# Gated linear attention and a GELU layer pair: the first rows through two hardware DMA queues, the weights behind a gate

## The chip, the cores and the metric

The kernel runs on one NeuronCore of a Trainium2 chip. The metric is the device time of one execution in microseconds (us), taken as the median over repeated runs. Engines are named as in the profile: PE (TensorE matmul) and PEld (its weight loads), DVE (VectorE), ACT (ScalarE), POOL (GpSimd) and SP (SyncE, which here only issues DMAs).

## The reference

A recurrent, gated linear attention is followed by two dense layers with a tanh GELU between them. B = 4 batches, H = 8 heads, S = 768 steps, D = 48; the layers go 384 to 2048 to 384. Inputs and output are float32.

```python
def _attn_ref(q, k, v, alpha):
    state = zeros(B, H, D, D); y = zeros_like(q)
    for t in range(S):
        state = alpha[:, :, t, :, None] * state + einsum('bhd,bhe->bhde', k[:, :, t], v[:, :, t])
        y[:, :, t] = einsum('bhd,bhde->bhe', q[:, :, t], state)
    return y

def reference(q, k, v, alpha, moe_w_in, moe_w_out):
    x = attn_out.transpose(0, 2, 1, 3).reshape(B * S, H * D)
    h = x @ moe_w_in
    g = 0.5 * h * (1.0 + tanh(sqrt(2 / pi) * (h + 0.044715 * h**3)))
    return g @ moe_w_out
```

## The kernel before

**Tiling.** The 768 steps are cut into 6 chunks of 128, and the 4 batches into 2 pairs, which gives 12 pairs (chunk, two batches), numbered 0 to 11 in the order of the chunks. For each pair four inputs are loaded: a (the decays alpha), q, k and v. One such load of one input is called a row here; it is 128 partitions by 16 heads by 48 numbers, 384 KB of float32 read in runs of 192 bytes. The v rows and the weights are cast to bfloat16 on the way, which the kernel does in DMAs of the software queue, issued by POOL.

**A pair's work.** ACT takes the logarithm of a (ln, L243). PE sums it over the steps (cum, L254 and L256), and ACT makes exp of the sum (b), of its negative (binv) and of its last row (bend). DVE scales q with b (qp) and k with binv (kp, L280). PE transposes both (qkT_ps, L291), they are copied to qkT (L305), and PE forms the scores (at, L327), which DVE masks (atm, L334). The product of kp and v (kv) updates the state (st). PE makes y from scores, v and state (yps), which is copied (x, L383), transposed (xT_ps, L390) and copied into xT (L394). Pairs 8 to 11 use DMA transposes instead of PE.

**The two layers.** For each pair, PE makes 16 groups of hT from w_in and xT (layer 1, L400), ACT applies the GELU (gT, L406), and PE sums over w_out into acc (layer 2, L414). The result is copied to ot (L421) and stored by SP (L426). Layer 1 of pair 0 is the first consumer of the weights. The groups of the two layers go in one fixed sequence (`stream`).

**What sets the order.** The program is scheduled by hand. `tasks` declares every step as a task with an engine, an estimated cost from the table `W`, a priority and its inputs and buffers; `Scheduler.order` then plays these through, always taking the task that can start first (within 60 ns, the one of the best priority), and the result is the fixed order of instructions on each engine. So a change of the loads' estimates also reorders the compute instructions. Where PE would idle in the first 60 us of that plan, a fill of matmuls on zeros is put in (L209). Tiles have numbered buffers in `BUFS`; `ca` is a single PSUM buffer that holds first cum and then the scores of each batch, so they take turns.

**The loads before.** `LOADS` lists the order: rows of pair 0, rows of pair 1, four parts of w_in, four parts of w_out, then the rows of pairs 2 to 11 (pair 2 in two halves). Only a of pair 0 is issued by SP, on a hardware queue; all the rest go through the software queue in this order. At most eight of the software loads are in flight, since each of eight semaphores is used again after its load has landed. `make_upper_triangular` (ut_h) and `make_identity` (ident) are built on POOL after its first and second load. `act_set` loads ACT's function table as ACT's first instruction.

Of the kernel before, what the change touches and what calls it, by code (L numbers as in the profile page):

```python
# [7 lines left out]
F32 = mybir.dt.float32  # L8
# [3 lines left out]
LN_EXP, GELU = 6, 0  # L12


W = dict(
    ln=760, exp=720, bend=170, gelu4=510, gelu2=340, table=1290,
    cum=530, t8=450, t4=225, attn=340, kv=170, inter=170, intra=205, tx=168, l1_4=655, l1_2=340, l2=655,
    qk2=910, qk1=500, ev8=650, ev4=350, mask=640, st=1400, st0=700, xc=520, xe=330, ot=540,
    ev8_act=960, ev4_act=520, xc_act=450, xe_act=450, ot_act=450,
    strip=2120, cast=1500, weight=1850, dma=2100, issue=1100, wissue=760, sp=100, store=2600, turn=1250, landed=2200, xbar_qk=1500, xbar_x=1000, first=3470, cold=500, fill=216, zero=1100,  # L20
)
LAT = {"SP": 0, "PE": 210, "ACT": 110, "DVE": 90, "POOL": 0}

# [1 line left out]
class Task:  # L25


    def __init__(self, kind, cost, prio, emit, deps=(), table=None, land=None, stream=None, xbar=0, late=0):
        self.kind, self.cost, self.prio, self.emit = kind, cost, prio, emit
        self.deps, self.takes = list(deps), []  # L30
        self.table, self.land, self.stream, self.xbar = table, land, stream, xbar
        self.late = late
        self.end = self.done = None
# [102 lines left out]
class _Kernel:  # L136
# [3 lines left out]

    SPLIT = (2,)
    EARLY = (0, 1)
    LOADS = ("0", "1", "in 0", "in 1", "in 2", "in 3", "out 0", "out 1", "out 2", "out 3",
             "2", "3", "4", "5", "6", "7", "8", "9", "10", "11")

    TURN_QK, TURN_X = (8, 9, 10, 11), (8, 9, 10, 11)
    BUFS = dict(ca=1, yk=2, ff=4, la=3, qp=4, kp=4, b8=2, qkT=4, atm=6, x=3, ot=6, bend=8,
                a=4, q=4, k=4, v=6)

    def __init__(self, ctx, tc, q, k, v, alpha, w_in, w_out, out):  # L150
        nc = self.nc = tc.nc
        self.tc, self.out = tc, out
        B, H, S, D = q.shape
        self.B, self.H, self.S, self.D = B, H, S, D
        C = self.C = 128
        self.NCH = S // C
        self.src = {"a": alpha, "q": q, "k": k, "v": v}
        self.w_in_dram, self.w_out_dram = w_in, w_out
        self.d_model, self.d_ff = w_in.shape
        self.NKT, self.NFT = self.d_model // C, self.d_ff // C  # L160

        self.const = ctx.enter_context(tc.tile_pool(name="const", bufs=1))
        self.sb = ctx.enter_context(tc.tile_pool(name="sb", bufs=1))
        self.ps = ctx.enter_context(tc.tile_pool(name="ps", bufs=1, space=bass.MemoryType.PSUM))

        const = self.const
        self.ut_h = const.tile([C, C], F16, name="ut_h")
        self.ut = const.tile([C, C], BF16, name="ut")
        self.ident = const.tile([C, C], BF16, name="ident")
        self.ones = const.tile([C, 1], F16, name="ones")  # L170
        self.zero = const.tile([C, 512], BF16, name="zero")
        self.w_in = const.tile([C, self.NKT, self.d_ff], BF16, name="w_in")
        self.w_out = const.tile([C, self.NFT, self.d_model], BF16, name="w_out")
        self.state = [[const.tile([C, H // 2, 2 * D], BF16, name=f"st{b}_{i}") for i in range(2)]
                      for b in range(B)]
        self.ring = {n: [const.tile([C, 2, H, 64], F16 if n == "la" else BF16, name=f"{n}{i}")
                         for i in range(self.BUFS[n])] for n in ("la", "qp", "kp")}
        self.used = {n: 0 for n in self.ring}
        self.xT = [const.tile([C, self.NKT, B, C], BF16, name=f"xT{c}") for c in range(self.NCH)]
        self.NG = 2  # L180
        self.gT = [const.tile([C, self.NFT, B * C], BF16, name=f"gT{i}") for i in range(self.NG)]
        self.eng = {"ACT": nc.scalar, "DVE": nc.vector}
# [30 lines left out]
    def load(self, n, c, i, lo=0, hi=2):  # L213

        nc, C, H, D = self.nc, self.C, self.H, self.D
        u = self.p[c, i]

        def emit(e):
            if n not in u:
                u[n] = self.tile(n, [C, 2, H, D], BF16 if n == "v" else F32)  # L220
            src = self.src[n][2 * i + lo:2 * i + hi].rearrange("b h s d -> s (b h) d")[c * C:(c + 1) * C]
            (nc.sync if e == "SP" else nc.gpsimd).dma_start(u[n][:, lo:hi].rearrange("t b h d -> t (b h) d"), src)  # L222
        return emit

    def load_w(self, which, part):
        def emit(e):
            if which == "in":
                w = self.d_ff // 4
                sl = slice(part * w, (part + 1) * w)
                self.nc.gpsimd.dma_start(  # L230
                    self.w_in[:, :, sl], self.w_in_dram.rearrange("(j c) n -> c j n", c=self.C)[:, :, sl])
            else:
                w = self.NFT // 4
                sl = slice(part * w, (part + 1) * w)
                self.nc.gpsimd.dma_start(
                    self.w_out[:, sl, :], self.w_out_dram.rearrange("(n c) p -> c n p", c=self.C)[:, sl, :])
        return emit
# [191 lines left out]
    def tasks(self):  # L429
        s = self.s = Scheduler(self.BUFS, self.fill, 60000)  # L430
# [3 lines left out]
        pairs = list(self.p)  # L434


        loads, n = {}, 0

        def load(key, cost, emit):
            nonlocal n  # L440
            land = W[{"v": "cast", "w": "weight"}.get(key[0], "strip")]
            loads[key] = s.add("load", {"POOL": cost}, n, emit, land=land // 2 if key[0] != "w" and key[1] in self.SPLIT else land)
            n += 1

        def rows(m, names="aqkv"):
            for lo, hi in self.parts(m):
                for r in names:
                    load((r, m, lo), W["issue"] * (hi - lo) // 2, self.load(r, *pairs[m], lo, hi))
                    loads[r, m, hi - 1] = loads[r, m, lo]

        def weights(which, parts):
            for part in map(int, parts):
                load(("w", which, part), W["wissue"], self.load_w(which, part))

        loads["a", 0, 0] = loads["a", 0, 1] = s.add("load", {"SP": 400}, 0, self.load("a", 0, 0), land=W["first"])
        for step in self.LOADS:
            if step == "0":
                rows(0, "qkv")
            elif step.isdigit():
                rows(int(step))  # L460
            else:
                weights(*step.split())
# [3 lines left out]
        for m, (c, i) in enumerate(pairs):  # L466
            u, P = self.p[c, i], 100 * m
# [3 lines left out]
            for lo, hi in self.parts(m):  # L471
                n = hi - lo
# [10 lines left out]
                step = 1 if early else n  # L483
# [12 lines left out]
            for j in range(2):  # L496
                b, o = 2 * i + j, P + 10 + 3 * j
                k = kp[j]
                if m not in self.TURN_QK:
                    turned = []  # L500
                    for which in ("q", "k") if early else ("qk",):
                        n = 4 * len(which)
                        cost = {"DVE": W[f"ev{n}"]}
# [42 lines left out]
        n = 0  # L546
# [45 lines left out]
    def run(self):  # L592
        nc = self.nc
        self.tasks()
        self.act_set(LN_EXP)
        nc.vector.memset(self.zero, 0.0)  # L596
        nc.vector.memset(self.ones, 1.0)
        first = [lambda: make_upper_triangular(nc, self.ut_h, val=1.0, diag=True), lambda: make_identity(nc, self.ident)]
        for i in range(max(self.BUFS[n] for n in self.ring)):
            for n in self.ring:  # L600
                if i < self.BUFS[n]:
                    nc.vector.memset(self.ring[n][i][:, :, :, self.D:64], 0.0)
        for b in range(self.B):
            for i in range(2):
                nc.vector.memset(self.state[b][i], 0.0)
        order = self.s.order()
        for t in order:
            if t.load == LN_EXP:
                self.act_set(LN_EXP)
            t.emit(t.engine)  # L610
            if t.kind == "load" and t.engine == "POOL" and first:
                first.pop(0)()
                if not first:
                    nc.vector.tensor_copy(self.ut, self.ut_h)
# [30 lines left out]
```

## Time and profile before

| | |
|---|---|
| median of 9 runs | 188.61 us (188.43 to 188.75) |
| the profiled execution | 188.43 us |
| its span in the profile | 186.7 us |
| PE busy | 175.4 us (94%) |
| ACT, DVE, POOL busy | 131.8, 104.3, 63.7 us |
| software DMA queue | 32464 packets, 19.27 MB |
| hardware DMA queue | 17296 packets, 8.00 MB |
| HBM read, written | 25.17 MB, 4.72 MB |

The span is what the profile shows of the program; the device time has another 1.7 us around it. Busy times of PE are modelled ends of pipelined matmuls, so that a busy PE can still have gaps; starts are the safer thing to read. The issue of a DMA is shown on its engine's queue (SPq, POOL), and the profile gives the time from issue to landing for each. In lines of the timeline the columns are start in us, duration in us, engine, line, operation, output and inputs, and in brackets the idle time before with what ended it.

### The profile page before, as it was taken

To read this page: it belongs to the slowest core of one execution; us is meant where nothing else is said; L and a number is where in the kernel's file an instruction comes from. 1 tells how busy PE (TensorE), PEld (TensorE's weight loads), DVE (VectorE), ACT (ScalarE), POOL (GpSimd) and SP (SyncE) were. 2 spreads that over 40 slices of the span, in tenths; PEclk is the share of its full clock that TensorE was granted. 3 is DMA by queue.
4 is the path that set the end of the run, shared out by engine and by line. 5 is a ranking of instruction groups with operands and counts; after the bars stand their busy time and mean duration, and the time that the engine had idled before them with its cause. 6 is when DMAs were issued, how large, how long until landed. Compare 5 with 4: busy or idle time off the path is not lost.

```text
span 186.7 us, 4504 instructions
## 1 busy us (share of the span) xinstructions
PE 175.4 (94%) x1831; PEld 126.5 (68%) x1834; DVE 104.3 (56%) x219; ACT 131.8 (71%) x297; POOL 63.7 (34%) x67
## 2 busy tenths in 40 slices
PE   5678899999999999999999999999999999999991
PEld 1344688556687787687688778677687687786850
DVE  7288640179687596597499798696645615000000
ACT  2635899743869769769799759788789884582911
POOL 7993543895556565565552200000000000000000
PEclk9999999999999999999999999999999999999998
DMA  6999999999999999999999997153270280301111
GB/s 130 177 183 168 205 204 213 199 180 238 233 218 184 153 227 205 171 237 197 177 221 217 188 208 139 43 126 77 42 181 20 52 187 15 101 14 47 42 42 44
DMA packets 49781, 27.56 MB, mean 148 GB/s; under 512 B 39744, under 2 KB 46400, under 8 KB 49760
## 3 DMA queue, kind: packets, MB, share of 16 engines
q0 software_dynamic: 32464, 19.27, 74.1%
q1 hardware_dynamic: 17296, 8.00, 17.7%
q8 instruction: 14, 0.23, 0.6%
q14 instruction: 7, 0.06, 0.1%
HBM read 25.17 MB, written 4.72 MB: 160 GB/s over the span
## 4 chain that ended last, share of the span: by engine, by line
PE 74%; DMA 13%; POOL 6%; ACT 2%; issue 1%; DVE 0%; POOLq 0%
PE acc L414 31%; PE hT L400 28%; DMA w_out<-in_moe_w_out_dram 8%; DMA a<-in_alpha_dram 6%; PE at L327 3%; PE qkT_ps L291 3%; PE yps L373 2%; PE yps L376 2%; PE cum L254 2%; POOL w_in L230 2%; PE kv L344 1%; POOL q L222 1%; POOL v L222 1%; POOL k L222 1%; PE xT_ps L390 1%
## 5 line engine op out<-in xcount | busy, mean ns | idle before, releaser
L406 ACT ACTIVATE gT<-hT 128x256 bf16<-128x256 f32 x192 | 63.5, 386 | 11.0 <-PE hT L400 10.5
L400 PE MATMUL hT<-xT,w_in 128*128 128x256 bf16 x576 | 69.9, 273 | 0.5 <-ACT gT L406 0.2
L414 PE MATMUL acc<-w_out,gT 128*128 128x384 bf16 x384 | 68.6, 326 | 0.0
L400 PEld LDWEIGHTS <-w_in 128*128 128x128 bf16 x576 | 54.2, 98 | 8.9 <-issue 0.8
L414 PEld LDWEIGHTS <-gT 128*128 128x128 bf16 x384 | 35.7, 97 | 20.4
L334 DVE TENSOR_TENSOR atm<-at,ut 128x512 bf16<-128x512 f32 x48 | 31.0, 685 | 13.8 <-PE at L327 12.9
L280 DVE TENSOR_TENSOR qp<-q,b 128x768 bf16<-128x768 f32 (+1 forms) x13 | 11.6, 891 | 18.9 <-ACT b L272 16.6
L421 ACT COPY ot<-acc 128x384 f32<-128x384 f32 x17 | 8.1, 479 | 18.6 <-PE acc L414 18.4
L222 POOL DMA_DIRECT2D k<-in_k_dram x13 | 14.5, 1113 | 11.9 <-DVE kp L280 4.8
L222 POOL DMA_DIRECT2D q<-in_q_dram x13 | 14.6, 1122 | 8.0 <-DMA q<-in_q_dram 2.8
L222 POOL DMA_DIRECT2D v<-in_v_dram x13 | 14.4, 1112 | 7.8 <-DMA a<-in_alpha_dram 2.8
L222 POOL DMA_DIRECT2D a<-in_alpha_dram x12 | 13.3, 1109 | 8.8 <-DMA k<-in_k_dram 3.0
L272 ACT ACTIVATE b<-cum 128x768 bf16<-128x768 f32 (+1 forms) x13 | 9.9, 762 | 7.4 <-PE cum L256 7.1
L243 ACT ACTIVATE la<-a 128x768 f16<-128x768 f32 (+1 forms) x13 | 10.2, 793 | 5.6 <-DMA a<-in_alpha_dram 5.5
L361 DVE TENSOR_TENSOR st<-stmp,bend 64x192 bf16<-64x192 f32 x32 | 11.3, 353 | 1.7
L200 ACT ACT_TABLE_LOAD x9 | 11.5, 1283 | 0.9 <-PEq L629 0.7
L280 DVE TENSOR_TENSOR kp<-k,binv 128x768 bf16<-128x768 f32 (+1 forms) x15 | 11.7, 791 | 0.8 <-DMA k<-in_k_dram 0.6
L359 DVE TENSOR_TENSOR stmp<-kv,st 64x192 f32<-64x192 f32 x32 | 11.3, 352 | 0.9 <-PE kv L344 0.6
L406 ACT ACT_TABLE_LOAD x9 | 11.5, 1283 | 0.2
L209 PE MATMUL idle<-zero 128*128 128x512 bf16 x31 | 9.8, 427 | 1.4 <-DVE zero L596 1.2
L383 DVE CAST x<-yps 128x384 bf16<-128x384 f32 x12 | 6.7, 556 | 7.6 <-PE yps L376 7.6
L305 DVE COPY qkT<-qkT_ps 128x1024 bf16<-128x1024 bf16 (+1 forms) x14 | 8.8, 649 | 3.5 <-PE qkT_ps L291 3.4
(43 smaller groups left out, 150.0 us busy)
## 6 DMA issues: line engine op xcount, KB each, us to landing
out_dram<-ot SPq DMA_DIRECT2D x24, 192.0 KB, 3.9
q<-in_q_dram POOLq DMA_DIRECT2D x11, 384.0 KB, 13.3
k<-in_k_dram POOLq DMA_DIRECT2D x11, 384.0 KB, 13.2
a<-in_alpha_dram POOLq DMA_DIRECT2D x10, 384.0 KB, 13.2
v<-in_v_dram POOLq DMA_DIRECT2D x11, 192.0 KB, 13.0
w_in<-in_moe_w_in_dram POOLq DMA_DIRECT2D x4, 384.0 KB, 11.6
w_out<-in_moe_w_out_dram POOLq DMA_DIRECT2D x4, 384.0 KB, 14.7
a<-in_alpha_dram SPq DMA_DIRECT2D x1, 384.0 KB, 4.0
```

Of the source, the lines that this page charges most:

```text
L200: nc.scalar.add_instruction(mybir.InstLoadActFuncSet(name=nc.get_next_instruction_name(), act_func_set_id=i, engine=mybir.EngineType.Activ ...
L209: self.nc.tensor.matmul(ps, self.zero[:, 0:self.C], self.zero, start=True, stop=True)
L222: (nc.sync if e == "SP" else nc.gpsimd).dma_start(u[n][:, lo:hi].rearrange("t b h d -> t (b h) d"), src)
L243: self.nc.scalar.activation(u["la"][:, lo:hi, :, 0:self.D], u["a"][:, lo:hi], AF.Ln)
L272: self.nc.scalar.activation(u[n].rearrange("t i h d -> t i (h d)")[:, lo:hi], u["cum"][:, lo:hi, 0:H * D], AF.Exp, scale=1.0 if n == "b" e ...
L280: self.nc.vector.tensor_tensor(u[n + "p"][:, lo:hi, :, 0:self.D], u[n][:, lo:hi], u["b" if n == "q" else "binv"][:, lo:hi], op=ALU.mult)
L334: self.nc.vector.tensor_tensor(u["atm", i][:, o], u["at", i][:, o], self.ut[:, None, :].to_broadcast([self.C, self.H // 2, self.C]), op=AL ...
L359: nc.vector.tensor_tensor(s[ps], acc, old[ps, :, fs], op=ALU.add)
L361: nc.vector.tensor_tensor(new[ps, :, fs], acc, u["bend"][ps, i, :, None].to_broadcast([64, H // 2, D]), op=ALU.mult)
L400: self.nc.tensor.matmul(h, self.w_in[:, j, nt * self.C:(nt + 1) * self.C], self.xT[c][:, j, lo:hi].rearrange("p g t -> p (g t)"), start=j ...
L406: return lambda e: self.nc.scalar.activation(self.gT[c % self.NG][:, nt, lo * self.C:hi * self.C], f.pop(("h", c, lo, nt)), AF.Gelu_apprx_ ...
L414: self.nc.tensor.matmul(f["acc", c, b], self.gT[c % self.NG][:, nt, b * self.C:(b + 1) * self.C], self.w_out[:, nt, :], start=nt == 0, sto ...
```

## The change

The six float rows of the first two pairs leave the software queue. `RINGS` gives each its issuer: SP issues a of pair 0, k of pair 0 and q of pair 1; ACT issues q of pair 0, a of pair 1 and k of pair 1. Each is one DMA over the whole pair. POOL issues v of pairs 0 and 1 first. Then a gate follows on POOL: two copies of one column each, out of k of pair 0 and a of pair 1 into a small tile, so that POOL goes on only when both have landed. All later loads, the weights first, are behind the gate. ACT's table load stands as a task after its second DMA, in place of the first instruction. In the table `W` the estimate of a weight load goes from 1850 to 2000, and rows on the hardware queues get 1500 and an issue cost of 450.

```diff
-    strip=2120, cast=1500, weight=1850, ..., first=3470, cold=500, fill=216, zero=1100,
+    strip=2120, cast=1500, weight=2000, ..., row=1500, row_issue=450, cold=500, fill=216, zero=1100,
...
-    LOADS = ("0", "1", "in 0", "in 1", "in 2", "in 3", "out 0", "out 1", "out 2", "out 3",
-             "2", "3", "4", "5", "6", "7", "8", "9", "10", "11")
+    LOADS = ('0', '1', 'gate', 'in 0', 'in 1', 'in 2', 'in 3', 'out 0', ..., '11')
+
+    RINGS = {('a', 0): 'SP', ('q', 0): 'ACT', ('k', 0): 'SP', ('a', 1): 'ACT', ('q', 1): 'SP', ('k', 1): 'ACT'}
+    GATE = (('k', 0), ('a', 1))
...
+        self.gate = const.tile([C, 2], F32, name="gate")
...
-            (nc.sync if e == "SP" else nc.gpsimd).dma_start(u[n][:, lo:hi].rearrange("t b h d -> t (b h) d"), src)
+            {"SP": nc.sync, "ACT": nc.scalar}.get(e, nc.gpsimd).dma_start(u[n][:, lo:hi].rearrange("t b h d -> t (b h) d"), src)
...
+    def wait(self, e):
+
+        pairs = list(self.p)
+        for j, (r, m) in enumerate(self.GATE):
+            self.nc.gpsimd.tensor_copy(self.gate[:, j:j + 1], self.p[pairs[m]][r][:, 0, 0, 0:1])
...
-            loads[key] = s.add("load", {"POOL": cost}, n, emit, land=...)
+            loads[key] = s.add("load", {"POOL": cost}, n, emit, [gate] if gate else [], land=...)
...
-        loads["a", 0, 0] = loads["a", 0, 1] = s.add("load", {"SP": 400}, 0, self.load("a", 0, 0), land=W["first"])
+        for (r, m), e in self.RINGS.items():
+            loads[r, m, 0] = loads[r, m, 1] = s.add("load", {e: W["row_issue"]}, n, self.load(r, *pairs[m]), land=W["row"])
+            n += 1
+            if n == 4:
+                s.add("table", {"ACT": W["table"]}, n, lambda e: self.act_set(LN_EXP))
         for step in self.LOADS:
             if step == "0":
-                rows(0, "qkv")
+                rows(0, "v")
+            elif step == "1":
+                rows(1, "v")
+            elif step == "gate":
+                gate = s.add("gate", {"POOL": 200}, n, self.wait, [loads[r, m, 0] for r, m in self.GATE])
...
-        self.act_set(LN_EXP)
```

Besides the loads, the order that the planner gives changes on PE, DVE and ACT. On PE four fills instead of six open the program. Seven fills follow the first cum, as before. The cum of pair 1 comes ahead of the second score product of pair 0, and on DVE the first state update comes ahead of the first masks. The sets of instructions on PE ahead of the first hT are otherwise the same.

## The prediction

> **What bounds the kernel now.** I read the chain of waits first. PE carries three quarters of it; the DMA and POOL shares all lie before 39 us, in loads.
> ```profile
> PE 74%; DMA 13%; POOL 6%; ACT 2%; issue 1%; DVE 0%; POOLq 0%
> ```
> Then busy times by stretch (columns: stretch, length, PE, PEld, DVE, ACT, POOL busy with counts, clock, DMA share, GB/s).
> ```profile
> 20.88:33.00 12.12, 12.11 (x128) 10.41 (x129) 4.61 (x11) 11.14 (x34) 5.54 (x7) 1.00 1.29 211
> 33.00:50.03 17.03, 16.11 (x159) 9.85 (x158) 10.76 (x23) 9.66 (x20) 13.00 (x12) 1.00 1.35 212
> 50.03:122.80 72.77, 72.77 (x842) 55.07 (x843) 55.73 (x112) 58.18 (x126) 29.90 (x26) 1.00 1.23 182
> 122.80:182.50 59.70, 59.48 (x568) 43.74 (x565) 19.28 (x34) 41.87 (x104) 0.00 (x0) 1.00 0.30 73
> ```
> From 20.88 us, where the first hT matmul (layer 1) starts, PE is full to 182.5 except in 33 to 50 us: 0.92 us idle and four fill matmuls, 4 x 0.216 = 0.86 us, so 1.8 us lost. The changed program has the same real PE work ahead of its first hT. The end therefore moves with **the start of layer 1**, less what those 1.8 us give back. So I read the timeline of the start.
> ```profile
> 0.74 0.46 SPq L222 DMA_DIRECT2D a<-in_alpha_dram  x1
> ...
> 4.76 0.84 ACT L243 ACTIVATE la<-a 128x768 f16<-128x768 f32 x1 [2.74 <-DMA a<-in_alpha_dram]
> ...
> 9.42 1.02 DVE L280 TENSOR_TENSOR kp<-k,binv 128x384 bf16<-128x384 f32 x2
> ...
> 17.60 0.35 DVE L394 COPY xT<-xT_ps 128x384 bf16<-128x384 bf16 x1
> ...
> 20.89 1.48 PE L400 MATMUL hT<-xT,w_in 128*128 128x256 bf16 x12 [0.17 <-DMA w_in<-in_moe_w_in_dram]
> ```
> The reader is to see two chains. The compute chain of pair 0, from a0 landing (4.74) by kp (9.42) to the last xT (17.95), is done 2.9 us before layer 1 starts; the transfer of w_in part 0 (lands 20.82) decides. It is late since the software queue moves its loads in order: a1 lands at 12.86, q1 15.0, k1 17.14, v1 18.5, so a float row takes 2.1 us and a v some 1.45. Last, the DMA view, 2.4 to 3.0 us (a0 alone, hardware queue) and 7.8 to 8.7 us (v, software queue).
> ```profile
> DMA packets 816, 0.16 MB, mean 261 GB/s; under 512 B 816, under 2 KB 816, under 8 KB 816
> q1 hardware_dynamic: 816, 0.16, 127.5%
> ...
> DMA packets 1249, 0.13 MB, mean 140 GB/s; under 512 B 1247, under 2 KB 1247, under 8 KB 1249
> ```
> 816 runs in 0.6 us are 1.36 per ns; v's 1249 in 0.9 us are 1.39. Two queues show one pace for 192-byte reads. A row of 2048 runs takes 1.5 us on the hardware queue. a0's first packet comes 1.16 us after issue (1.9 us) and its landing some 0.95 us after its last packet (3.8 us).
>
> **What the Trainium skill says.** "DMA: Bandwidth & Descriptors" (Queues, rings and completion order): each DMA engine takes packets round robin from the queue rows that have work; rows of different issuers do not add engines. The trace agrees as far as it goes: a0's tail with q0 (3.4 to 3.6 us) is 224 runs plus 4 packets of 16 runs, 1.44 per ns, only 6% above one queue. "Perfetto Trace Analysis" (DMA Instruction, HWDGE): the issuer holds the descriptor generator until all descriptors are made, and engines start early where their buffer fills. The trace shows 0.46 us for a0's issue, and no two such loads in a row. "TensorE: Matmul & The Clock Gate" (What's actually happening): after an idle window of about 3.4 us PE runs at half its clock, until a window of work has passed. The first six fills stand 0.427 us apart, the seven from 6.18 us 0.216.
>
> **The change, part by part.**
>
> *Two rows at once.* a0 goes out on SP and q0 on ACT together, and v0 by POOL at 1.28, with packets from 3.4 us as q0 has now. At 1.4 runs per ns, 4096 runs of a0 and q0 shared alike, and v0 with a third of the turns from 3.4, end at 5.7; a0 lands at 6.6. If the generator serves SP first, a0 leads by 0.46 us and lands near 5.9. I take 6.2: **1.5 us later than now**. From a0 to kp takes 9.42 - 4.74 = 4.7 us, with nothing removed, so kp can start at 10.9.
>
> *k0 and a1.* They follow on the same rings. By 3.4 us some 2000 runs have moved; the other 6200 at two thirds of 1.43 per ns take 6.5 us, end 9.9, land 10.9 (9.0 if v got no turns, 11.9 if v went wholly ahead). k0 is thus 1.6 us later than its 9.3, just in time for kp at 10.9; a1 is 2 us earlier. q1 and k1 land by 14.4 (all 16384 runs at 1.43 per ns end at 13.4): used from 16.3 on, so hidden.
>
> *From kp to layer 1.* The new order has pair 1's cum and exps ahead of pair 0's second score (at). Counted from kp: transposes, copy, at 1.8; st for b0, now ahead of the masks, to 2.4; masks 1.29 to 3.7; cum, b, binv, bend 2.3 (14.95 to 17.23 now) to 6.0. DVE then runs without a gap: qp 0.96, xT 0.35, half a kp 0.5, to 7.3; masks 1.29 to 8.6; kp 0.5, st 0.73, one mask 0.65, xT 0.35 to 10.8. First hT at kp + 10.9 = **21.8, 0.9 later than 20.88**. Today it is 8.5 from kp to the last xT; the extra 2.3 is pair 1's part moved ahead.
>
> *Clock.* Four fills now open instead of six: PE is busy 1.19 to 2.9, then idle to cum, a0 + 0.9 = 7.1, which is 4.2 us. Cold, the seven fills behind cum cost 7 x 0.211 = 1.5 us more, cum some 0.4, of which about 0.6 is slack before qp is ready: 1.3 if cold throughout, 0 if warm, and below nothing is excluded, as no clock above the full one appears. The window may end within the fills, so I take 1.0. Layer 1: +1.9.
>
> *Gate.* Two POOL copies of 128x1, not in the trace; nearest are POOL memsets of 0.10 and 0.22 us, so 0.2 to 0.45. Behind them on POOL wait the eight weight loads, then every load from pair 2 on. Weights issue at 11.2 instead of 10.52. No engine is idle for it: q1, k1 and v1 move to 13.4, and w_in's packets come 2.1 us after issue, at 13.3. w_in part 0 needs 1.9 us (the spacing of weight landings now) and lands at 16.2 instead of 20.82; the last w_out some 13 us later, as now, 29.2 instead of 33.8. The cover is 5 us; if it went, layer 1 would wait for weights as now.
>
> *Issues.* Five POOL issues of 1.15 us go, 5.75 us in all, which gains nothing by itself as the engines' pace is the limit. SP issues k0 and q1 ahead of its first store at 38.6: free. ACT issues q0, a1, k1 at 0.46 each, with the table load (1.28) behind two of them; even with six issues in one line (6 x 0.46) all is done at 3.5, before ln at 6.2.
>
> *What comes back.* Pair 2's loads come some 4 us earlier. Now ln waits for them 0.9 us and kp 0.6 in 33 to 50 us. The new order has five fills there, 1.1 us, and more of pair 3 between: 1.8 - 1.1 = 0.7 back at best, nothing at worst; I take 0.6. Later stretches are full and keep their length.
>
> **Sum:** 1.9 - 0.6 = +1.3 us. The profiled execution took 188.43 us (span 186.70 plus 1.73 around it), 0.18 below the median 188.61: 189.7 on its own time, **189.9** on the median.
>
> **The rivals.**
>
> *A, faster: two rings outrun one.* If one ring and not the engines gave 1.36 runs per ns, two might give 1.9. Then a0 lands at 1.9 + 4096/1900 + 0.95 = 5.0, PE idles 3 us and stays warm, kp at 9.7, layer 1 at 20.6 (-0.3), and the 0.6 comes back: 187.7. For it: the share of 127% shows packets overlapping. Against: v's equal pace and the 6% of the mixed stretch. It decides from a0 landing before 5.3, where kp + 10.9 falls to 20.88. Chance 0.19.
>
> *B, much slower: ACT is held in its issues.* If a ring can't take a second row until the first has moved, a1's issue holds ACT to 5.7, the table load follows, k1's issue holds it to about 10, and ln of pair 0, queued behind, starts 3.8 us later: some 193.5. For it: buffers that fill. Against: a0's issue ended 0.7 us before its first packet, so one row at least is taken at once. Chance 0.10.
>
> *C, a draw:* v takes few turns, PE stays warm, and all 0.7 us come back: 188.6. Chance 0.08.
>
> **Numbers.** The forecast has 0.63, its own range 188.9 (warm: +0.9 - 0.6) to 191.2 (a0 at 6.6, cold throughout, nothing back: +2.6). Slower is forecast plus B, 0.73; same is C; faster is A, 0.19. 0.2% is about what a measurement can tell here. The range of 187.6 to 192.0 takes in A's value and leaves out B.
>
> **What would show it.** a0's landing (ln's start) near 6.2, together with q0; k0 and a1 near 11; fills spaced 0.427 after cum; w_in landed long before the first hT, whose wait names DVE's xT; first hT near 22.8; fewer waits on loads at 33 to 50 us. A first hT before 20.9 or ln before 5.3 makes the forecast wrong; ACT issues of several us would be B.

## The result, and the profile after

The changed kernel takes **189.86 us** (median of 10 runs, 189.52 to 190.39) against 188.66 (31 runs) for the kernel before: 1.0068 times, with a 95% interval of 1.0060 to 1.0076. Its profiled execution took 189.55 us, with a span of 187.8 us (before: 188.43 and 186.7). The chain of waits no longer has any load in it.

```profile
PE 85%; ACT 4%; DVE 2%; issue 1%
```
```profile
23.79:33.00 9.21, 9.21 (x108) 8.08 (x106) 3.27 (x7) 8.94 (x25) 4.42 (x5) 1.00 1.30 218
33.00:50.03 17.03, 17.03 (x171) 11.78 (x171) 9.55 (x19) 11.85 (x28) 13.11 (x12) 1.00 1.31 226
50.03:122.80 72.77, 72.33 (x842) 54.79 (x841) 53.95 (x112) 58.59 (x125) 29.09 (x26) 1.00 1.06 176
122.80:184.39 61.59, 61.38 (x580) 44.73 (x578) 21.17 (x36) 43.00 (x106) 0.00 (x0) 1.00 0.30 73
```
The second fence is the busy time by stretch, with the columns as in the prediction. From the first hT to the last ot it takes 160.60 us, where before it took 182.50 - 20.89 = 161.61. So 1.01 us come back. In 33 to 50 us PE is now busy for all 17.03 us, but only half of the old hole is closed; the other half has moved. Of the 0.92 us idle before, 0.5 us were waits for the sums of pair 2, whose logarithm waited for its rows:
```profile
35.10 0.52 ACT L243 ACTIVATE la<-a 128x384 f16<-128x384 f32 x1 [0.49 <-DMA a<-in_alpha_dram]
...
39.01 0.52 ACT L243 ACTIVATE la<-a 128x384 f16<-128x384 f32 x1 [0.45 <-DMA a<-in_alpha_dram]
```
These waits are gone. The other 0.4 us stood beside four fills from 48.3 us on; the same four now start from 50.2 us on, with 0.44 us of idle PE in the third line. Over the whole way from the first hT to the last ot PE idles 1.14 us before (161.61 less 160.47 busy) and 0.65 after (160.60 less 159.95). So half of the 1.01 us is less idling, and half is less busy time.

The start must have lost more than comes back. The timeline of the start shows how.

```profile
1.25 1.89 ACTq L225 DMA_DIRECT2D a<-in_alpha_dram  x1
...
3.20 4.27 ACTq L225 DMA_DIRECT2D k<-in_k_dram  x1
7.51 0.84 ACT L252 ACTIVATE la<-a 128x768 f16<-128x768 f32 x1 [3.06 <-issue]
8.40 0.48 PE L263 MATMUL cum<-la,ut_h 128*128 128x384 f16 x1 [5.32 <-ACT la L252]
...
9.26 3.03 PE L212 MATMUL idle<-zero 128*128 128x512 bf16 x7
...
12.12 0.61 PE L300 MATMUL qkT_ps<-ident,qp 128*128 128x128 bf16 x8
...
12.53 0.18 POOL L232 COPY gate<-k 128x1 f32<-128x1 f32 x1 [7.72 <-DMA k<-in_k_dram]
...
12.77 0.42 DVE L314 COPY qkT<-qkT_ps 128x512 bf16<-128x512 bf16 x1 [1.54 <-PE qkT_ps L300]
...
13.11 1.02 DVE L289 TENSOR_TENSOR kp<-k,binv 128x384 bf16<-128x384 f32 x2
```
Read these lines from the top. ACT's third row, k1, holds ACT in its issue from 3.20 to 7.47 us; a0 had landed at 5.74 (0.74 plus the 5.0 that the trace gives for it), but ln, behind that issue on ACT, starts at 7.51. The bracket says "issue", not a DMA. The seven fills stand 0.43 us apart, so the transposes of qp behind them start only at 12.12. The gate's first copy shows k0 landing just before 12.53. kp starts at 13.11, behind DVE's copy of those transposes; before, it started at 9.42. So three things are late by themselves: ln, the fills, and k0. The first hT follows at 23.79:

```profile
22.83 0.35 DVE L403 COPY xT<-xT_ps 128x384 bf16<-128x384 bf16 x1
...
23.79 0.82 PE L409 MATMUL hT<-xT,w_in 128*128 128x256 bf16 x6
```
There is no wait for w_in in it: w_in part 0 landed at about 18.8 (issue at 13.64, and 5.2 us to landing, the shortest of the four parts). Why k0 came so late is seen in the DMA view, first from 5 to 7 us and then from 7 to 10:
```profile
DMA packets 2503, 0.31 MB, mean 157 GB/s; under 512 B 2503, under 2 KB 2503, under 8 KB 2503
...
q0 software_dynamic: 1700, 0.16, 153.0%
q1 hardware_dynamic: 335, 0.06, 29.3%
q10 hardware_dynamic: 468, 0.09, 26.4%
```

```profile
DMA packets 3153, 0.50 MB, mean 168 GB/s; under 512 B 3153, under 2 KB 3153, under 8 KB 3153
...
q1 hardware_dynamic: 1051, 0.20, 60.9%
q0 software_dynamic: 1051, 0.10, 60.7%
q10 hardware_dynamic: 1051, 0.20, 32.8%
```
SP's ring is q1, ACT's is q10 (a ring is the queue of one issuer), and v's software queue is q0. From 7 us on the three took turns exactly alike, and together moved 3153 runs in 3 us, 1.05 per ns. From 5 to 7 us it was worse: v came in and took two thirds of the packets, from 5.5 to 6.0 us 753 of 754, while a0 and q0 had ended and k0 and a1 hardly moved. The same comes with v in other kernels: with six rows on one ring from 3.8 to 4.6 us (757 of 805 packets are v's), and where v is issued later, from 7.8 to 8.4 us (835 of 858). Why the rings stand still while v comes in was not found. The turns from 7 us on explain the rest of k0's delay: its 2048 runs, one in three of 1.05 per ns, take 5.9 us.

The third place is the end. From the start of the last ot to the end of the span it takes 186.7 - 182.50 = 4.2 us before and 187.8 - 184.39 = 3.4 us after. In the last 2.7 us of the kernel before, the DMA view has, besides the store, one fetch of instructions, which the one after does not have there:

```profile
q1 hardware_dynamic: 108, 0.14, 14.5%
q14 instruction: 1, 0.01, 1.2%
```
**The account:** the first hT 2.90 later, 1.01 back between it and the last ot, 0.8 back at the end: +1.1 us of span, and 189.55 - 188.43 = 1.12 measured in the profiled executions.

### The profile page after: what moved, and what is told of

The parts are those of the page before. It is cut to its first block, busy times and chain, and to the rows that moved or that the text cites. A ratio compares the mean times of both kernels' runs of the same rounds, so it can differ in the third digit from the quotient of the medians.

```text
span 187.8 us, 4506 instructions
## 1 busy us (share of the span) xinstructions
PE 174.9 (93%) x1828; PEld 127.1 (68%) x1831; DVE 102.6 (55%) x216; ACT 133.6 (71%) x300; POOL 58.8 (31%) x64
## 3 DMA queue, kind: packets, MB, share of 16 engines
q1 hardware_dynamic: 21424, 8.79, 20.2%
## 4 chain that ended last, share of the span: by engine, by line
PE 85%; ACT 4%; DVE 2%; issue 1%
PE hT L409 33%; PE acc L423 32%; PE at L336 4%; PE qkT_ps L300 3%; PE yps L385 2%; PE cum L263 2%; PE yps L382 2%; PE kv L353 2%; PE xT_ps L399 2%; ACT qkT L314 2%; PE cum L265 1%; PE idle L212 1%; DVE atm L343 1%; ACT L415 1%; ACT ot L430 1%
## 5 line engine op out<-in xcount | busy, mean ns | idle before, releaser
L225 POOL DMA_DIRECT2D k<-in_k_dram x11 | 12.1, 1103 | 11.4 <-DVE kp L289 5.2
L225 POOL DMA_DIRECT2D q<-in_q_dram x11 | 12.1, 1103 | 8.1 <-DVE qp L289 4.2
L225 POOL DMA_DIRECT2D a<-in_alpha_dram x11 | 12.2, 1110 | 4.7 <-DMA k<-in_k_dram 1.4
L263 PE MATMUL cum<-la,ut_h 128*128 128x384 f16 x24 | 7.4, 337 | 5.4 <-ACT la L252 5.3
L392 ACT CAST x<-yps 128x384 bf16<-128x384 f32 x14 | 6.7, 479 | 6.3 <-PE yps L385 6.1
```

Of the source, the lines that this page charges most:

```text
L225: {"SP": nc.sync, "ACT": nc.scalar}.get(e, nc.gpsimd).dma_start(u[n][:, lo:hi].rearrange("t b h d -> t (b h) d"), src)
L263: nc.tensor.matmul(cum[:, i, 0:H * D], self.ut_h, la[:, i, :, 0:D], start=True, stop=True)
```

## The experiments

Each was timed in five rounds beside the kernel before, whose median was 188.66 to 188.79 in these sets; the ratio is against the kernel before of the same set. The edits are against the kernel after, unless said otherwise. "Start" is the start of the first hT, "middle" the time from there to the start of the last ot. These columns are from one profiled execution each. Those of "six rows on one ring" and "no gate" contain a stretch in which the clock granted to PE was half, of which more below.

| kernel | median us | ratio to before, 95% | ln | kp | start | middle |
|---|---|---|---|---|---|---|
| before | 188.66 | 1 | 4.76 | 9.42 | 20.89 | 161.61 |
| after | 189.86 | 1.0068 (1.0060 to 1.0076) | 7.51 | 13.11 | 23.79 | 160.60 |
| k1 on SP | 189.23 | 1.0024 (1.0016 to 1.0033) | 5.82 | 12.69 | 23.38 | 160.60 |
| 14 opening fills | 189.37 | 1.0036 (1.0022 to 1.0050) | 7.50 | 12.83 | 23.52 | 160.61 |
| both of these | 190.33 | 1.0081 (1.0056 to 1.0105) | 5.77 | 12.65 | 23.34 | 160.60 |
| both, v1 behind the gate | 188.35 | 0.9977 (0.9966 to 0.9989) | 5.75 | 11.38 | 22.07 | 161.40 |
| six rows on one ring | 189.81 | 1.0052 (1.0037 to 1.0068) | 4.54 | 12.70 | 24.42 | 160.64 |
| one ring, both v later | 188.86 | 1.0016 (1.0001 to 1.0030) | 4.45 | 9.37 | 21.54 | 161.96 |
| no gate | 197.54 | 1.0462 (1.0432 to 1.0493) | 7.70 | 13.83 | 31.53 | 162.00 |
| loads after, order before | 190.12 | 1.0079 (1.0063 to 1.0094) | 7.64 | 12.95 | 24.08 | 160.73 |
| loads before, order after | 187.62 | 0.9941 (0.9929 to 0.9953) | 4.47 | 10.37 | 21.05 | 160.67 |
| the same, 8 opening fills | 187.87 | 0.9953 (0.9941 to 0.9965) | 4.45 | 10.58 | 21.26 | 160.62 |

**The hold of ACT: k1 issued by SP.**
```diff
+    ISSUE = {('k', 1): 'SP'}
...
         def emit(e):
+            e = self.ISSUE.get((n, 2 * c + i), e)
```


> One edit to the changed kernel: k of pair 1 is issued by SP behind its other three rows, so that ACT issues two rows, not three. Theory L (two limits in a row): ln of pair 0 starts at a0's landing, near 5.8 instead of 7.5, but kp then waits for k0, which still lands near 12.5; kp near 12.6 instead of 13.1, time 189.3 us. Rival H (ACT's hold in the issue is the whole matter): everything moves by 1.7 us, time near 188.1.

With two rows on ACT, ln starts at 5.82 instead of 7.51, and what it waits for is the DMA of a: the hold was the whole of the 1.7 us. But kp moves by 0.4 only, since it now waits for k:
```profile
12.69 1.03 DVE L291 TENSOR_TENSOR kp<-k,binv 128x384 bf16<-128x384 f32 x2 [0.66 <-DMA k<-in_k_dram]
```
So the hold is real, and most of it lies beside the late k0, as theory L had it. It costs 0.6 us between the medians (189.86 to 189.23), and 0.42 between the profiled executions (189.55 to 189.13), as much as kp moves. What makes the third issue so long is less sure. ACT's runs until 7.47 us and SP's third until 6.86, so a part of ACT's may be a wait for SP's. With one ring and no issue on ACT, below, the third still takes 3.10 us.

**The cold PE: 14 opening fills in place of 4.**
```diff
-            for _ in range(n):
+            for _ in range(14 if first else n):
```


> One edit to the changed kernel: the opening has 14 fill matmuls instead of 4, so that PE idles for less than 3 us ahead of cum. Theory L: the seven fills behind cum stand 0.216 us apart instead of 0.427, the transposes of qp start near 11.0 instead of 12.1, kp near 12.6, held by k0; time 189.3 us. Rival N (PE's clock is hidden behind ACT or the loads): time unchanged, 189.9. Rival C (the clock alone): kp 0.94 us earlier, 188.9.

cum takes 0.32 us each, not 0.48, and qp starts 0.34 earlier, at 9.93. kp again meets k:
```profile
12.83 1.03 DVE L291 TENSOR_TENSOR kp<-k,binv 128x384 bf16<-128x384 f32 x2 [0.80 <-DMA k<-in_k_dram]
```
It gains 0.5 us between the medians, 0.26 between the profiled executions.

**Both edits together, run twice.**

> Both edits together: k of pair 1 on SP, and 14 opening fills. Theory L (k0's landing near 12.5 is the next limit): kp near 12.6, time 189.3 us, no better than either edit alone. Rival (the two costs add, k0 is no limit): kp near 10.5, first hT near 21.2, time near 187.3.

> The same kernel as the one with k1 issued by SP and 14 opening fills, whose profiled execution took 189.12 us where its timed runs had a median of 190.33. If the profiled execution is the typical one, 189.1 to 189.4 us; if the timed runs are, 190.3.

The start of the first profiled execution is as expected from a k0 at 12.6: kp waits 2.34 us for it, first hT at 23.34, 189.12 us. But the median was 190.33 in the first set and 190.69 in the second. The second profile shows why. Here are busy times by stretch of 2 us (PE, PEld, DVE, ACT, POOL, clock, DMA share, GB/s), 14 to 16 us, of the 189.12 us execution and then of one with 190.31 us:
```profile
14.00:16.00 2.00, 1.92 (x21) 0.93 (x20) 1.86 (x5) 1.61 (x3) 2.00 (x4) 1.00 1.31 249
```
```profile
14.00:16.00 2.00, 1.84 (x18) 1.08 (x18) 1.34 (x4) 1.18 (x3) 2.00 (x3) 0.50 1.31 247
```
The clock granted to PE was halved in part of 12 to 18 us, after PE had stood idle from about 10.9 to 13.3 waiting for k. kp starts alike in both (12.65 and 12.71); the first hT is 1.20 us later, the time 1.19. The mean granted clock is 0.989 or 0.990 in the four timed runs of 190.26 to 190.52 us and 0.982 in that of 191.21, so 190.3 or more is the typical time of this kernel. What decides whether an idle stretch is followed by the half clock was not found: PE idles 2.77 us ahead of kp's transposes in the execution without it and 2.48 in the one with it.

**v's turns: v1 behind the gate, with both edits above.**
```diff
-            t.emit(t.engine)
+            if t is self.v1:
+                pass
+            else:
+                t.emit(t.engine)
+            if t.kind == "gate":
+                self.v1.emit("POOL")
```


> As the kernel with k of pair 1 on SP and 14 opening fills, and v of pair 1 issued behind the gate, so that only v of pair 0 shares the engines with the rows. Theory L: k0 lands near 11.8 instead of 12.5, kp near 11.9, time 0.6 us below that kernel, 188.7 us. Rival (k0 is no limit, or v takes no turns): no change against that kernel.

k0 lands at 11.34 instead of about 12.6, and the first hT moves by as much, from 23.34 to 22.07:
```profile
11.38 1.03 DVE L293 TENSOR_TENSOR kp<-k,binv 128x384 bf16<-128x384 f32 x2 [0.77 <-DMA k<-in_k_dram]
```
That is 0.5 us earlier than expected. A row that nobody needs yet took turns from the one that was waited for. The middle is 0.8 us longer (161.40): PE idles 1.29 us in it, 0.57 of that in one wait for a logarithm of pair 2, which waits 0.99 us for its row. The start came 1.7 us earlier than in the kernel after, but the weights, with the later rows behind them, were issued when they are there (13.56 against 13.64). The medians of this kernel and the one with both edits alone lie further apart than that (188.35 and 190.33). The profiled executions, both at the full clock, differ by 0.48 us (188.64 and 189.12), which is 1.27 less 0.80. The rest is probably the half clock: 11 of the 12 executions of the other kernel have a mean clock of 0.990 or less, and one of nine here.

**One ring in place of two.**
```diff
+    ISSUE = {(r, m): 'SP' for r in 'aqk' for m in (0, 1)}
```


> One edit to the changed kernel: all six rows are issued by SP, in the order a0, q0, k0, a1, q1, k1, so that they move one after the other and ACT issues none. Theory R (rows that run side by side land together, late; in a line the first ones land early): a0 at 4.8, k0 near 9.3, kp 9.5 to 10.4 (the higher with PE at half clock), a1 near 12.7, first hT 20.3 to 21.1, time 187.0 to 188.0 us. Rival (the engines' pace and v's turns alone decide when k0 lands): k0 near 12, time near 189.5.

This prediction of mine fell; the rival came true. a0 is early (ln at 4.54), but q and k are not:
```profile
9.26 0.96 DVE L291 TENSOR_TENSOR qp<-q,b 128x768 bf16<-128x768 f32 x1 [4.76 <-DMA q<-in_q_dram]
...
12.70 1.03 DVE L291 TENSOR_TENSOR kp<-k,binv 128x384 bf16<-128x384 f32 x2 [1.33 <-DMA k<-in_k_dram]
```
The DMA view from 7 to 10 us has two queues there, with about half of the packets each:
```profile
q0 software_dynamic: 2092, 0.20, 124.9%
q1 hardware_dynamic: 1899, 0.36, 67.5%
```
Together they move 1.33 runs per ns, but only 0.63 are float rows; with two rings it was 2 x 0.35 = 0.70. With fewer rings v holds a larger share. The start of 24.42 holds one thing more. This execution had the half clock from about 13.3 to 16.3 us, and from kp to the first hT it took 11.72 us, where the kernel after takes 10.68. Three of the six executions have a mean clock of 0.988 and took 190.1 to 190.2 us; the three at full clock took 189.25 to 189.52.

**One ring, v0 behind a0 and v1 behind the gate, 10 opening fills.** The edits for the ring and the fills are as above, and ut_h and ident are built first.
```diff
-            t.emit(t.engine)
...
+            if t is self.v[0]:
+                nc.gpsimd.tensor_copy(self.gate[:, 0:1], ... ["a"][:, 0, 0, 0:1])
+            if t is not self.v[1]:
+                t.emit(t.engine)
+            if t.kind == "gate":
+                self.v[1].emit("POOL")
```


> All six float rows go out on SP in the order a0, q0, k0, a1, q1, k1; v of pair 0 is issued by POOL behind a copy of one column of a0, v of pair 1 behind the gate, ahead of the weights; 10 opening fills in place of 4. Theory T (the equal turns that v takes on the engines set when q0 and k0 land; with v out of the way the rows follow at some 1.36 runs per ns): ln at 4.5, q0 lands about 6.2 and k0 about 7.7, so that kp no longer waits for k (kp near 9.4 with a warm PE), first hT near 20.2, 186.3 us in all with a tail of 3.4 us. Rival U (it is SP's own issues that hold the rows back, each behind room in the one ring): q0 and k0 land near 9.2 and 12.7 as with v in the way, first hT near 24, 189.5 us.

For kp the first theory holds to 0.1 us: it starts at 9.37 and waits for no load, as k0 lands by 8.8 without v in the way. That is a microsecond later than the 7.7 expected, since the ring alone moved 1.20 runs per ns (5524 from 2.4 to 7 us) and not 1.36. For the start (21.54, expected near 20.2) it does not hold, and the working shows the omission: v0 and a1 are needed next, and come late in their turn (PE waits for v0, ACT for a1, whose issue ended at 6.69):
```profile
11.78 0.34 PE L357 MATMUL kv<-v,kp 128*128 128x96 bf16 x4 [1.41 <-DMA v<-in_v_dram]
...
12.44 0.84 ACT L256 ACTIVATE la<-a 128x768 f16<-128x768 f32 x1 [1.45 <-DMA a<-in_alpha_dram]
```
Also the middle is 1.4 us longer than that of the kernel after, with 1.25 us of PE idle in 33 to 50 us.

**The gate taken out** (its task stays, its two copies go).
```diff
-                gate = s.add("gate", {"POOL": 200}, n, self.wait, ...)
+                gate = s.add("gate", {"POOL": 200}, n, lambda e: None, ...)
```


> One edit to the changed kernel: the two gate copies on POOL are left out. Theory W (the gate has slack: the weights stand behind both v loads in the software queue anyway, and layer 1 does not wait for them): w_in lands some 2 us earlier, q1 and k1 up to 1.5 us later but in time, time 189.9 us within 0.3. Rival (without it the weights take turns from k0 and a1): k0 1 us or more later, time 190.8 or more. Rival (the gate costs): 189.4 or below.

It costs 7.7 us against the kernel after, where I had expected next to nothing. The DMA view from 16 to 20 us:
```profile
q0 software_dynamic: 580, 0.56, 83.1%
q1 hardware_dynamic: 585, 0.11, 25.0%
q10 hardware_dynamic: 581, 0.11, 13.6%
```
The packets are again shared alike, but one of the software queue's is now a piece of a weight with 0.56 MB / 580, about 970 bytes, where one of a float row has 192. (The view counts bytes as they are written, after the cast; by that count a v packet had 96.) So q1 and k1 get a third of the packets each and a seventh of the bytes; q1 lands at 25.0, and pair 1 waits for it:
```profile
25.03 0.96 DVE L289 TENSOR_TENSOR qp<-q,b 128x768 bf16<-128x768 f32 x1 [6.17 <-DMA q<-in_q_dram]
```
In the kernel after, the gate lets v and the rows run ahead; from 14 to 16 us the two rings move 2665 runs and the software queue 25 packets.

The late q1 is not all of the cost. PE idles from 20.1 to 26.0 us, and the clock granted to it is half from about 24.4 to 34.6. All six executions show a low mean clock (0.974 to 0.983). The profiled one, 9.14 us longer than that of the kernel after, divides as follows: this qp starts 6.83 us later (25.03 against 18.20), the way from it to the first hT takes 0.91 longer (6.50 against 5.59), and the middle 1.40 (162.00). So about three quarters are the late row itself. The other 2.3 us fit the half clock, which came with the idling: it covers all of that way and the first 3.1 us of the middle, where half of the time would be 1.5 us (an estimate).

**Loads and order apart.** The planner's order and the loads change together. In one kernel the loads of after are written out ahead of the order of before, in the other the loads of before ahead of the order of after. The edit of the second, against the kernel after, is shown; that of the first is its mirror, against the kernel before:
```diff
+        for r, m in (("a", 0), ("q", 0), ("k", 0), ("v", 0), ("a", 1), ("q", 1), ("k", 1), ("v", 1)):
+            rows[r, m].emit("SP" if (r, m) == ("a", 0) else "POOL")
...
         for t in order:
+            if t in rows.values() or t.kind in ("gate", "table"):
+                continue
```


> The loads of the changed kernel, the compute order of the kernel before. Theory S (the late start is in the loads, ACT's hold and PE's half clock; the new order itself costs nothing): ln of pair 0 near 7.5 us, kp near 13.1. In the order of before PE needs 11.3 us from kp to the first hT (9.42 to 20.72, with pair 1's pieces ahead of it in PE's queue), so first hT near 24.4, and with some 0.8 us given back 191.1 us. Rival O (the new order, with pair 1's sums ahead of pair 0's second scores, costs 2.3 us between kp and layer 1): first hT near 21.7, time near 188.4.

> The loads of the kernel before, the compute order of the changed kernel. Theory S: ln at 4.76, kp at 9.42, then the order waits some 1.5 us on a1 (12.86) and k1 (17.14), first hT near 21.6, and with about 0.5 us given back 188.6 us (188.2 to 189.0). Rival O (the order costs the time): near 189.9. Rival G (the new order is what gives time back after 33 us, 1.0 us or more): 187.6 or below.

The new loads with the old order give the late start (24.08) and the short middle (160.73); the time is 1.0 us below the 191.1 that theory S gave, as kp came early, the middle gave more back and the end was shorter. The new order with the old loads gives an early start and the short middle too, and is **faster than both kernels**: 187.62 us, 0.9941 times before (0.9929 to 0.9953).
```profile
21.05 0.82 PE L409 MATMUL hT<-xT,w_in 128*128 128x256 bf16 x6
...
181.72 0.48 ACT L430 COPY ot<-acc 128x384 f32<-128x384 f32 x1 [2.08 <-PE acc L423]
```
This is close to rival G. Either part alone brings about what both bring: 0.88 us by the loads, 0.94 by the order, 1.01 together. Both fill the same hole: over the whole middle PE idles 1.14 us before, 0.63 with the loads alone, 0.66 with the order alone and 0.65 with both. Either way its waits for the sums of pair 2 are gone. The rest, 0.4 to 0.5 us of PE's busy time in the middle (160.47 before, 160.10, 160.01 and 159.95), is not resolved further.

> The loads before with the order after, and 8 opening fills in place of 4. Theory T (kp is ruled by PE's clock until then, layer 1 by the landing of w_in part 0 at 20.8): kp moves from 10.37 to about 9.4, the first hT only from 21.05 to about 20.85, 187.4 us in all, a difference of 0.1%. Rival U (layer 1 follows kp by 10.7 whatever w_in does): first hT at 20.1 and 186.7 us.

The eight fills did not make PE warm. They ended at 4.8, and cum at 5.34 still took 0.48 each; the fills behind it stood 0.43 apart up to 8.7. kp came at 10.58, and the first hT 10.68 us after it, at 21.26. Without the fills it was also kp + 10.68 (10.37, 21.05). In both the first hT follows kp by the same time, so the compute chain, not w_in, seems to set the start in this kernel as it stands. This is rival U's reading, though not its number: kp did not come earlier, and what a kp at 9.4 would bring was not seen.

## Why the prediction was right, and where its steps were not

The sign and the cause, a later layer 1, were right, and so was the time (189.9 against 189.86). That the time was hit so closely is luck: the start was missed by +1.0 us, the middle by -0.4 and the end by -0.8, and these cancel. Term by term:

- **a0's landing:** forecast 6.2, measured 5.74 (+1.0 instead of +1.5).
- **Issues on ACT:** the forecast had 0.46 each and ACT free at 3.5; they took 0.48, 1.89 and 4.27 us. This is rival B in kind, with a chance of 0.10: it took one row more to fill than that rival supposed, so that ln lost 1.77 us instead of 3.8. The step that failed is pricing the second and third row at the issue of the first; 0.46 us was no bound for three. "Perfetto Trace Analysis" (DMA Instruction, HWDGE) in the Trainium skill says that the issuer holds the generator until all descriptors are made. The trace agrees as far as it goes: ACT was held for 4.27 us, and k1's issue ended when about 2350 of the 6144 runs of ACT's ring had moved, so that about 3800 were still to go, an estimate of 237 for each of 16 engines.
- **k0's landing:** forecast 10.9, with bounds of 9.0 to 11.9; measured 12.5. The step that failed is "6200 runs at two thirds of 1.43 per ns". Two thirds was right on the mean (6365 of the 9816 runs from 3.4 to 12 us were float rows), but not as equal turns: v had no packet until 5.0 us, then nearly all, then a third. The pace was not right: two queues do 1.295 per ns (2331 runs in 3.2 to 5 us), three do 1.05, and the mean was 1.14. Rival A falls by the first of these numbers: two rings do not outrun one.
- **The clock:** +1.0 forecast. ln to kp takes 5.60 us against 4.66, +0.94. Right in size, but with k0 behind it the clock alone was worth less: 14 fills brought kp forward by only 0.28.
- **kp to the first hT:** 10.9 forecast, 10.68 measured. Right in size. But the forecast took this for 2.3 us more than the chain of before, and the old order with the new loads takes 11.13: the new order shortens this way. So of the 2.90 us at the start, 3.69 lie ahead of kp (9.42 to 13.11), and the new path from kp to hT gives 0.8 back against the 11.47 of before.
- **What set layer 1 before:** I read 2.9 us of slack in the compute chain and took w_in to decide. The wait of 0.17 us on w_in was real, but in PE's fixed order pair 1's pieces (at, kv) stand ahead of the first hT, and they ran until 20.72. Both ended together, so an earlier w_in alone would have brought some 0.17 us (an estimate from that wait; it was not tried). The last xT was the wrong line to read as the end of the chain.
- **The gate:** costed at nothing behind 5 us of cover. It is that, but the cover is not all that it gives: without it, 7.7 us are lost. "DMA: Bandwidth & Descriptors" (Queues, rings and completion order) says that engines take packets round robin from the queues; where all three queues were moving, the runs agree to 1% in packets (1051 each; 580, 585 and 581). I used this for v and not for the weights, whose packets are five times as large as a float row's (970 bytes and 192).
- **Weights:** w_in part 0 forecast at 16.2, at about 18.8 in the trace. Without effect, as hT came later.
- **What comes back:** 0.6 forecast, 1.01 measured. The reason given, pair 2's loads 4 us earlier, was off: the second half of pair 2's v is issued at 34.09 instead of 34.30; it is layer 1 that moved 2.9 us closer to it. Nor were there five fills in 33 to 50 us: four run from 50.2 us on.
- **The end:** forecast as unchanged, 0.8 us shorter. This was in no step.

Removing the hold or the cold clock brings 0.6 and 0.5 us (189.23, 189.37), as k0 is next in both cases, at about 12.6. Removing a part of k0's delay too, by v1, brings the next 1.3 us of the start.

## What to carry to other kernels

Ahead of the first work, count packets, not bytes: where three queues here had work, each took an equal turn, so a row that is not needed yet, or a queue with larger packets, delays the one that is waited for. A second ring added no pace (1.30 runs per ns against 1.20 to 1.36 for one). Put long issues on an engine with nothing else to do, and price an issue by how much already lies in its ring. And where a change of loads makes a planner reorder the work as well, run the two apart: here the order was worth 0.6% and the loads, alone, cost 0.8%.

## What the runs showed of the hardware that was not expected

- Three queues with 192-byte runs moved 1.05 per ns, where two moved 1.30 to 1.33 and one 1.20 to 1.36. While v's queue came in, the rings all but stopped for 0.6 to 1 us.
- An issue of a row of 2048 runs took 0.46 to 0.48 us as the first in a ring, 1.27 to 1.89 as the second, 4.27 and 4.28 as the third in the kernel after, 3.10 as the third on one ring, and 1.79 as the third on the one ring that v had not yet joined. During each of these four third issues about one row moved on the same ring (1923, 1759, 1983 and 2097 runs), which fits a ring that takes about two rows and makes the third wait for room.
- The granted clock fell to 0.5 in some executions of a kernel and not in others, after PE had idled: for some 3.4 us in the kernel with both edits and in the one with six rows on one ring (with 2.5 and 1.8 us of idling), and for about 10 us without the gate (it fell 4.3 us into an idle stretch). What decides it is open. In the slow fills at the start the same column reads 1.00, so whether the two have one cause is open too. The moment at which opening fills make PE fast varies too: after 14 fills from 1.19 us, one execution has them 0.22 apart from about 5.0 on, another has all of them 0.43 apart. With eight fills PE stayed slow until after 9 us, though it idled no longer than 0.56 us from 1.19 on.
- The span after the last ot's start is 4.1 to 4.2 us in the three kernels with the loads of before, with an instruction fetch in it in each, and 3.3 to 3.4 us in the ten executions with the new loads, which have no fetch there. That the fetch is the cause was not tried.
